# An attention and feed-forward kernel: weight pieces behind the seven-product tiles loaded and converted in halves

## The chip, the cores and the metric

The kernel runs on one core of one Trainium2 chip. The metric is the device time of one execution in microseconds (us), lower is better. The kernel before takes 477.06 us (median of three runs, 477.06 to 477.33). A profiled execution of it, from which all rows below come, took 475.99 us; its span, from the first to the last instruction, is 474.2 us.

## The reference

Three layers follow each other. Inputs of the attention are float32, the weights of the two feed-forward layers are float64.

```python
# attention: 2 x 12 heads, 448 tokens, 64 wide
scores = cap * np.tanh(scale * np.matmul(q, k.transpose(0, 1, 3, 2)) / cap)
attn = exp(scores - max) / (sum + 1e-09);  x = np.matmul(attn, v)   # -> 896 x 768
# first feed-forward layer, w_in 768 x 1024, w_out 1024 x 768
h = x @ w_in;  solu = h * softmax(h);  x = layernorm(solu) * g_ln @ w_out
# second feed-forward layer, w_gate and w_val 768 x 1536, w_out 1536 x 768
g = x @ w_gate
silu = g * (1.0 / (1.0 + np.exp(-g)))
val = x @ w_val
return (silu * val @ w_out).astype(np.float32)
```

The change lies in the second feed-forward layer alone.

## The kernel before

Matrix products work on float32 numbers that are split into a high and a low part: ACT copies the number into the rounded type (`hi_act`), DVE subtracts the copy from the number (`lo_dve`). A product of two such pairs is three matmuls (`mm3`: high by high, high by low, low by high). `split` in the code is the pair hi_act and lo_dve.

A float64 weight comes from memory as 64-bit raw words. `load_shifted` loads them three bytes off, so that the byte with sign and exponent and the word below lie aligned, and `f32_shifted` makes a float32 of them in three steps: a first Prelu on ACT (from the top byte, read as int8), a second Prelu on ACT in place (written as int32), and one SCALAR_TENSOR_TENSOR on DVE, the fill, that brings in the mantissa's bits. An older way, `load64` and `f32`, takes one Abs on ACT and four instructions on DVE, two TENSOR_SCALAR and two SCALAR_TENSOR_TENSOR.

Of the 12 tiles of the second layer's hidden width (fc = 0 to 11, 128 columns of w_gate and w_val each), tiles 1 to 8 are computed with seven products instead of eight on blocks; their order on every engine is written out by hand. Behind them the tiles 9, 10 and 11 are plain: for each of the two token ranges (384 and 512 columns), 18 matmuls for the gate product, 18 for the value product, a Silu on ACT, a product on DVE and a split. There only TensorE's order is fixed by the code; that of ACT and DVE is set by a scheduler when the program is built.

Beside these three tiles the kernel loads what is still missing: the two weights of tile 11 (`load_gv`), and from the second layer's w_out (names `w2_...`) nine pieces (`load_w2`). A piece with a number under 6 is 128 rows of all 768 columns: its left half is split into B11, and right minus left is kept as T1f. Pieces 6, 8 and 10 are the left halves of two chunks each and are split into B21. `early` says which pieces are asked for in which half of which tile. Every piece has 768 words in each of 128 partitions, one raw buffer (tag `raw`, two buffers) and one float32 buffer (tag `f32`, two buffers). All loads are issued in order by SP.

Then `ff2_out` computes the output, again with fewer block products: units named p1, p5, p2 and so on, 18 matmuls of 384 columns each, for token blocks 0, 1, 2 and 6. p1 multiplies A11 by B11, p2 multiplies A12 by B21, p5 works on the sums S1 and T1, p6 on S2 and T2. S2 is written over S1 (tile `so`) by three splits. Beside the first units the right halves of w_out2's lower chunks, three pieces b22, are loaded (`load_b22`, the same two raw buffers), converted the older way (`f32_b22`) and split (`split_b22`); T2, T3, S2 and so on are formed from them and others on DVE, then split.

In the rows, `g` is a weight buffer of gate, value or B parts, `w_raw` a raw w_out2 piece, `b` the float32 b22, `a` the hidden tile and the B22 parts, `p` an accumulator or an output row, `so` the sums S and T. Since a helper records every instruction, all have line L49 in the profile.

Of the kernel before, what the change touches and what calls it, by code (L numbers as in the profile page):

```python
# [5 lines left out]
F32 = mybir.dt.float32  # L6
F32R = mybir.dt.float32r
U32 = mybir.dt.uint32
I64 = mybir.dt.int64
# [47 lines left out]
class Kernel:  # L57
# [566 lines left out]
    def load_gv(self, fc, i):  # L624

        if fc not in self.gvs:
            self.gvs[fc] = [self.g4[m].rearrange("p (u k f) -> p u k f", u=2, f=128)
                            for m in (((0, 1), (2, 3))[fc % 2] if fc else (2, 1))]
        n, w, d = "gv"[i], (self.w_gate, self.w_val)[i], self.gvs[fc][i]
        src = w[:, fc * 128:(fc + 1) * 128].rearrange("(k p) f -> p k f", p=128)  # L630
        raw = self.ee[:, :1536].bitcast(I64) if fc == 0 and i else None
        raw = self.load_shifted(src, f"w{n}_{fc}", raw)
        f = self.f32_shifted(raw, f"w{n}_{fc}").rearrange("p (k f) -> p k f", k=self.KD)
        self.hi_act(d[:, 0], f)
        self.lo_dve(d[:, 1], f, d[:, 0])

# [297 lines left out]
    def split(self, d, src):  # L934

        self.hi_act(d[0], src)
        self.lo_dve(d[1], src, d[0])

    def load_w2(self, fc):

        n = self.HN
        if fc >= self.KD:
            src = self.w_out2[fc * 128:(fc + 2) * 128, :n].rearrange("(f p) d -> p f d", p=128)
        else:
            src = self.w_out2[fc * 128:(fc + 1) * 128, :]
        f = self.f32_shifted(self.load_shifted(src, f"w2_{fc}"), f"w2_{fc}").rearrange("p (f d) -> p f d", f=2)
        if fc >= self.KD:
            for m in range(2):
                self.split(self.B21[fc - self.KD + m], f[:, m])
        else:  # L950
            self.split(self.B11[fc], f[:, 0])
            if fc == len(self.T1f):
                self.T1f.append(f[:, 1])
            self.V.tensor_tensor(self.T1f[fc], f[:, 1], f[:, 0], op=ALU.subtract)

    def load_b22(self, k):

        src = self.w_out2[(self.KD + k) * 128:(self.KD + k + 2) * 128, self.HN:].rearrange("(f p) d -> p f d", p=128)
        self.b22raw[k] = self.load64(src, f"b22_{k}")

    def f32_b22(self, k):

        f = self.B22f[:, k:k + 2].rearrange("p f d -> p (f d)")
        self.f32(self.b22raw.pop(k), f"b22_{k}", f=f)

    def split_b22(self, k):

# [179 lines left out]
    def run(self):  # L1147
# [18 lines left out]
        w = [self.w_in_steps(i) for i in range(KD)]  # L1166
        f, g, hi, lo = zip(*w)
        self.w_steps = [((), f[0][:1], ()), (f[0][1:2], (), f[0][2:] + g[0][:1]), ((), (g[0][1], hi[0]), (lo[0],))]
        for i in range(1, KD):
            a = g[i][:1]  # L1170
# [9 lines left out]
        h = [self.ff1_h(t) for t in range(7)]  # L1180
# [9 lines left out]
        st = self.pool("st", side="right")  # L1190
# [21 lines left out]
        steps = h[1] + h[2][:1] + T[0] + h[2][1:] + h[3][:1] + T[1] + h[3][1:] + wo[0] + h[4][:2] + T[2] + h[4][2:] + wo[1] + h[5][:5] + T3 + h[5][5:] + h[6][:-1] + T4 + h[6][-1:]  # L1212
# [3 lines left out]
        n = self.HN = self.DM // 2  # L1216
        wb, gb = self.wb, _ = self.pool("wb"), self.pool("gb")
# [8 lines left out]
        steps = x2[0][0] + x2[0][1] + wo[2] + x2[1][0][:1] + T5 + x2[1][0][1:] + x2[1][1] + T6  # L1226
        steps += wo[3] + x2[2][0][:1] + x2[0][2] + x2[1][2] + [(0.0, lambda j=j: self.x_sums0(j)) for j in J[:2]]
        for j in range(2, KD):
# [4 lines left out]
            a, b = x2[j]  # L1233
# [27 lines left out]
        self.sg = (self.ee[:, :n], self.ee[:, n:n + 512])  # L1261
        self.T1f = [self.ee[:, n + 512 + n * i:n + 512 + n * (i + 1)] for i in range(3)] + [t1, self.sms]
        self.t1 = t1
        early = {9: ((6, 8), (0,)), 10: ((1,), (2,)), 11: ((3, 4), (5, 10))}
        for fc in range(K2):
            if fc == 0:
                self.ff2_gv_first()
                self.ff2_gv_sevens()
            if fc <= self.KS:
                continue  # L1270
            self.pinned = (nc.tensor,)
            if fc == self.KS + 1:
                d = self.S3f[:, 4:]
                self.V.tensor_tensor(d, d, self.S1f[:, 4:], op=ALU.subtract)
                xR = wb.tile([128, 2688], F32R, name="kR", tag="xR")
                self.B21p[0] = two(xR[:, :1536])
                self.B21[:2] = both(self.B21p[0])
                self.B11[2] = tuple(xR[:, 1536 + n * u:1536 + n * u + n] for u in range(2))
            for i, (N, o) in enumerate(((n, 0), (512, n))):
                if fc == self.KS + 1:  # L1280
                    for m in "hl":
                        self.steps[fc + 1]["GV"[i] + m]()
                elif fc + 1 < K2:
                    self.load_gv(fc + 1, i)
                for c in early[fc][i]:
                    self.load_w2(c)
                self.ff2_gv(fc, N, o)
# [46 lines left out]
```

## Time and profile before

| what | us |
|---|---|
| median of the runs | 477.06 |
| profiled execution | 475.99 |
| its span | 474.2 |
| TensorE (PE) busy | 466.7 (98%) |
| DVE busy | 387.8 (82%) |
| ACT busy | 310.4 (65%) |
| GpSimd (POOL) busy | 38.7 (8%) |

TensorE's granted clock is full in all 40 slices of the span. A busy share is an average over the whole span; in the changed stretch, from about 345 us on, each engine has another share, and the section of rows shows them. A wait in a row stands in brackets: how long the engine was idle just before the instruction, and which engine and tile ended that.

### The profile page before, as it was taken

The numbers are of one execution on the slowest core, as the hardware profiler recorded it, in microseconds if no ns is written. First come the engines' busy times: TensorE is split into PE (matmuls) and PEld (weight loads), VectorE is DVE, ScalarE is ACT, GpSimd is POOL, SyncE is SP. The second block draws the span as 40 slices with busy tenths as digits, with TensorE's granted clock in tenths as the row PEclk, the third lists the DMA queues.
The fourth block names the chain that finished last, engine by engine and source line by source line (L and its number), as shares of the span: only waits on it lengthen the run. The fifth ranks groups of instructions, "written<-read, shape, count | busy, mean of one in ns | idle before, by whom it ended". The sixth has DMA issues, their size and how long they took to land.

```text
span 474.2 us, 7675 instructions
## 1 busy us (share of the span) xinstructions
PE 466.7 (98%) x2970; PEld 384.8 (81%) x2970; DVE 387.8 (82%) x669; ACT 310.4 (65%) x455; POOL 38.7 (8%) x76
## 2 busy tenths in 40 slices
PE   9999999999999999999999999999999999998997
PEld 7444454447888899989989999999999889998996
DVE  3689999987778996866778899989876768999993
ACT  4999999951223799887767766766667778344220
POOL 1011010112000000000012222220000000000000
PEclk9999999999999999999999999999999999999999
DMA  6786575002000225345225444331445757010003
GB/s 181 170 207 153 163 193 153 21 2 88 1 1 0 90 88 165 126 129 180 66 81 185 134 134 132 109 122 37 132 128 155 241 182 221 7 50 18 17 19 132
DMA packets 65060, 52.33 MB, mean 110 GB/s; under 512 B 35584, under 2 KB 61952, under 8 KB 64256
## 3 DMA queue, kind: packets, MB, share of 16 engines
q1 hardware_dynamic: 64992, 51.85, 36.7%
q8 instruction: 23, 0.38, 0.3%
q14 instruction: 13, 0.11, 0.1%
q0 software_dynamic: 32, 0.00, 0.0%
HBM read 49.09 MB, written 2.75 MB: 109 GB/s over the span
## 4 chain that ended last, share of the span: by engine, by line
PE 80%; DVE 10%; DMA 5%; ACT 4%; issue 1%; ACTq 0%; DVEq 0%; SPq 0%
PE x L49 12%; PE h L49 12%; PE p L49 8%; PE g L49 8%; PE pv L49 8%; PE sc L49 7%; PE b L49 6%; PE c L49 6%; PE S L49 4%; DMA w_raw<-in_moe_w_out_dram 3%; PE e L49 3%; DVE b L49 2%; ACT w L49 2%; PE v L49 2%; DVE so L49 1%; PE lt L49 1%
## 5 line engine op out<-in xcount | busy, mean ns | idle before, releaser
L49 PE MATMUL g<-x,g 128*128 128x448 f32 (+2 forms) x288 | 62.2, 365 | 0.0
L49 PE MATMUL h<-wi,x 128*128 128x512 f32 x252 | 59.2, 393 | 0.0
L49 PEld LDWEIGHTS g<-x,g 128*128 128x128 f32 x288 | 53.1, 188 | 5.4 <-ACT ee L49 0.3
L49 PEld LDWEIGHTS h<-wi,x 128*128 128x128 f32 x252 | 46.8, 188 | 11.3 <-issue 1.5
L49 ACT ACTIVATE P<-sc,consts 112x896 f32<-112x896 f32 x48 | 45.4, 1010 | 3.8 <-PE sc L49 2.2
L49 ACT ACTIVATE P<-P,consts 112x3584 f32<-112x3584 f32 (+1 forms) x13 | 39.7, 3060 | 0.1
L49 PE MATMUL pv<-P,v 112*32 112x448 f32 x384 | 38.5, 540 | 0.0
L49 PEld LDWEIGHTS sc<-ks 64*112 64x112 f32 x288 | 23.3, 171 | 18.3 <-issue 8.4
L49 PE MATMUL sc<-ks 64*112 64x448 f32 x288 | 35.8, 379 | 0.3
L49 PE MATMUL x<-lB,wo 128*128 128x256 f32 (+1 forms) x192 | 35.2, 337 | 0.0
L49 PEld LDWEIGHTS x<-lB,wo 128*128 128x128 f32 x192 | 29.6, 189 | 3.4
L49 PE MATMUL b<-a,g 128*128 128x448 f32 x144 | 31.9, 366 | 0.0
L49 ACT ACTIVATE ee<-h,sms 128x512 f32<-128x512 f32 x14 | 9.5, 685 | 33.2 <-DVE sms L49 33.2
L49 PEld LDWEIGHTS pv<-P,v 112*32 112x32 f32 x384 | 12.2, 110 | 23.0 <-issue 20.9
L49 PE MATMUL v<-x,g 128*128 128x384 f32 (+1 forms) x144 | 30.4, 362 | 0.3 <-DVE g L49 0.3
L49 PEld LDWEIGHTS b<-a,g 128*128 128x128 f32 x144 | 27.0, 188 | 2.3 <-DVE ee L49 0.2
L49 PEld LDWEIGHTS v<-x,g 128*128 128x128 f32 x144 | 26.0, 188 | 3.5 <-DVE g L49 0.7
L49 PE MATMUL x<-lA,wo 128*128 128x384 f32 x144 | 27.2, 338 | 0.0
L49 PEld LDWEIGHTS x<-lA,wo 128*128 128x128 f32 x144 | 25.2, 188 | 0.5
L49 POOL COPY sm<-tr 32x14 f32<-32x14 f32 x48 | 15.0, 312 | 93.1 <-DVE tr L49 91.6
L49 PE MATMUL S<-P,ones 112*32 112x448 f32 x192 | 22.4, 549 | 0.0
L49 DVE TENSOR_TENSOR x<-x,x 128x448 fp32r<-128x448 f32 (+3 forms) x26 | 15.3, 588 | 8.3 <-ACT x L49 7.6
(273 smaller groups left out, 967.6 us busy)
## 6 DMA issues: line engine op xcount, KB each, us to landing
wg_raw<-in_moe_w_gate_dram SPq DMA_DIRECT2D x12, 765.8 KB, 4.3
wv_raw<-in_moe_w_val_dram SPq DMA_DIRECT2D x11, 765.8 KB, 4.7
wi_raw<-in_moe_w_in_dram SPq DMA_DIRECT2D x6, 1024.0 KB, 7.7
w_raw<-in_moe_w_out_dram SPq DMA_DIRECT2D x6, 767.6 KB, 4.2
wo_raw<-in_moe_w_out_dram SPq DMA_DIRECT2D x6, 512.0 KB, 3.5
wo_raw<-in_moe_w_out_dram SPq DMA_DIRECT2D x6, 510.5 KB, 3.6
v<-in_v_dram SPq DMA_DIRECT2D x24, 112.0 KB, 4.0
kq<-in_k_dram SPq DMA_DIRECT2D x22, 112.0 KB, 3.0
```

Of the source, the lines that this page charges most:

```text
L49: i = f(*a, **k)
```

## The change

Behind the seven-product tiles the two raw tiles are taken once, as four halves of 384 words. `load_halves` loads a piece in two loads, each into the next of the four halves, and converts each half by itself: two Prelus and a fill over 384 columns each. The float32 buffer is still one of 768 columns, and the splits that follow are as before. Both `load_w2` and `load_gv` for tile 11 use it. `early` asks for the pieces in another order. The three b22 pieces are loaded shifted and converted by two Prelus and one fill of 768 columns, no longer by Abs and four DVE instructions.

```diff
@@ load_gv
-        raw = self.ee[:, :1536].bitcast(I64) if fc == 0 and i else None
-        raw = self.load_shifted(src, f"w{n}_{fc}", raw)
-        f = self.f32_shifted(raw, f"w{n}_{fc}").rearrange("p (k f) -> p k f", k=self.KD)
+        if fc:
+            f = self.load_halves([src[:, 3 * h:3 * h + 3] for h in range(2)], f"w{n}_{fc}")
+        else:
+            raw = self.ee[:, :1536].bitcast(I64) if i else None
+            f = self.f32_shifted(self.load_shifted(src, f"w{n}_0", raw), f"w{n}_0")
+        f = f.rearrange("p (k f) -> p k f", k=self.KD)
@@ new
+    def load_halves(self, src, name):
+
+        f = self.st[0].tile([128, 768], F32, name=name, tag="f32", bufs=2)
+        steps = [{}, {}]
+        for h in range(2):
+            raw = self.halves.pop(0)
+            self.halves.append(raw)
+            self.load_shifted(src[h], f"{name}_{h}", raw)
+            self.shifted_steps(steps[h], "", lambda raw=raw: raw, lambda h=h: f[:, 384 * h:384 * h + 384])
+        for o in steps:
+            for w in "12f":
+                o["w" + w]()
+        return f
@@ load_w2
-        n = self.HN
+        n, w = self.HN, self.w_out2
         if fc >= self.KD:
-            src = self.w_out2[fc * 128:(fc + 2) * 128, :n].rearrange("(f p) d -> p f d", p=128)
+            src = [w[(fc + h) * 128:(fc + h + 1) * 128, :n] for h in range(2)]
         else:
-            src = self.w_out2[fc * 128:(fc + 1) * 128, :]
-        f = self.f32_shifted(self.load_shifted(src, f"w2_{fc}"), f"w2_{fc}").rearrange("p (f d) -> p f d", f=2)
+            src = [w[fc * 128:(fc + 1) * 128, h * n:(h + 1) * n] for h in range(2)]
+        f = self.load_halves(src, f"w2_{fc}").rearrange("p (f d) -> p f d", f=2)
@@ load_b22, f32_b22
-        self.b22raw[k] = self.load64(src, f"b22_{k}")
+        self.b22raw[k] = self.load_shifted(src, f"b22_{k}")
-        self.f32(self.b22raw.pop(k), f"b22_{k}", f=f)
+        raw, o = self.b22raw.pop(k), {}
+        self.shifted_steps(o, "b", lambda: raw, lambda: f)
+        for w in "12f":
+            o["wb" + w]()
@@ run
-        early = {9: ((6, 8), (0,)), 10: ((1,), (2,)), 11: ((3, 4), (5, 10))}
+        early = {9: ((0, 1), (2,)), 10: ((3,), (6,)), 11: ((4, 8), (5, 10))}
...
+                self.halves = [t[:, a:a + 384] for t in (st.tile([128, 768], I64, name=f"h{m}", tag="raw", bufs=2)
+                                                         for m in range(2)) for a in (0, 384)]
```

The load queue, SP, from behind the last load of the seven-product tiles to the last w_out2 piece, before (`w_6_raw` is the raw buffer of piece 6, `wg_raw` and `wv_raw` those of tile 11's gate and value weights):

```order
L177 DMA w_6_raw<-in_moe_w_out_dram 128x2x3069
L177 DMA w_8_raw<-in_moe_w_out_dram 128x2x3069
L173 DMA w_0_raw<-in_moe_w_out_dram 128x6141
L177 DMA wg_raw<-in_moe_w_gate_dram 128x6x1021
L173 DMA w_1_raw<-in_moe_w_out_dram 128x6141
L177 DMA wv_raw<-in_moe_w_val_dram 128x6x1021
L173 DMA w_2_raw<-in_moe_w_out_dram 128x6141
L173 DMA w_3_raw<-in_moe_w_out_dram 128x6141
L173 DMA w_4_raw<-in_moe_w_out_dram 128x6141
L173 DMA w_5_raw<-in_moe_w_out_dram 128x6141
L177 DMA w_10_raw<-in_moe_w_out_dram 128x2x3069
```

The same place now; `h_3484` and `h_3485` are the two raw tiles, each of two halves, and the pieces are 0, 1, 2, gate, 3, value, 6, 4, 8, 5 and 10:

```order
L173 DMA h_3484<-in_moe_w_out_dram 128x3069 x2
L173 DMA h_3485<-in_moe_w_out_dram 128x3069 x2
L173 DMA h_3484<-in_moe_w_out_dram 128x3069 x2
L177 DMA h_3485<-in_moe_w_gate_dram 128x3x1021 x2
L173 DMA h_3484<-in_moe_w_out_dram 128x3069 x2
L177 DMA h_3485<-in_moe_w_val_dram 128x3x1021 x2
L173 DMA h_3484<-in_moe_w_out_dram 128x3069 x2
L173 DMA h_3485<-in_moe_w_out_dram 128x3069 x2
L173 DMA h_3484<-in_moe_w_out_dram 128x3069 x2
L173 DMA h_3485<-in_moe_w_out_dram 128x3069 x2
L173 DMA h_3484<-in_moe_w_out_dram 128x3069 x2
```

Eleven loads have become 22; the value weights of tile 11 are sixth and piece 5 is tenth in both.

DVE at piece 5, beside the last value product (`v_384`), before (`w_5` is the float32 piece, `g_0_1928` the buffer of B11's chunks 4 and 5):

```order
L49 SCALAR_TENSOR_TENSOR w_5_3784<-w_5_raw,w_5_3784 128x768
L49 TENSOR_TENSOR w_5_3784<-w_5_3784 128x384
L49 TENSOR_TENSOR ee<-v_384_3820,ee 128x512
L49 TENSOR_TENSOR g_0_1928<-w_5_3784,g_0_1928 128x384
L49 TENSOR_TENSOR s_2487<-s_2487,ee 128x384
```

And now:

```order
L49 SCALAR_TENSOR_TENSOR w_5_3811<-h_3485,w_5_3811 128x384
L49 TENSOR_TENSOR g_0_1928<-w_5_3811,g_0_1928 128x384
L49 TENSOR_TENSOR w_5_3811<-w_5_3811 128x384
L49 SCALAR_TENSOR_TENSOR w_10_3823<-h_3484,w_10_3823 128x384 x2
L49 TENSOR_TENSOR g_1_1929<-w_10_3823,g_1_1929 128x384 x2
L49 TENSOR_TENSOR ee<-v_384_3855,ee 128x512
```

The low part of piece 5 comes right behind its second fill, and piece 10 is done ahead of the eviction of the last value product.

DVE at the second and third b22 piece, before (`b_3850` is the float32 b22, `a_2485` its split parts):

```order
L49 TENSOR_TENSOR so<-sms,so 128x384
L49 TENSOR_TENSOR g_1_1929<-w_10_3793,g_1_1929 128x384 x2
L49 TENSOR_TENSOR so<-w_5_3784,so 128x384
L49 TENSOR_SCALAR b_3850<-b_3850 128x768 x2
L49 SCALAR_TENSOR_TENSOR b_3850<-b_2_raw,b_3850 128x768 x2
L49 TENSOR_SCALAR b_3850<-b_3850 128x768 x2
L49 SCALAR_TENSOR_TENSOR b_3850<-b_4_raw,b_3850 128x768 x2
L49 TENSOR_TENSOR a_2485<-b_3850,a_2485 128x2x384 x3
```

And now:

```order
L49 TENSOR_TENSOR so<-sms,so 128x384
L49 TENSOR_TENSOR so<-w_5_3811,so 128x384
L49 SCALAR_TENSOR_TENSOR b_3885<-b_2_raw,b_3885 128x768
L49 SCALAR_TENSOR_TENSOR b_3885<-b_4_raw,b_3885 128x768
L49 TENSOR_TENSOR a_2485<-b_3885,a_2485 128x2x384 x3
```

Each piece has one DVE instruction in place of four; behind the three splits the order of DVE is the same as before.

## Rows read from the trace of the kernel before

**Rows 1.** TensorE in order of time: start, us, instruction [idle before, released by].
```profile
377.05 0.52 PE L49 MATMUL v<-x,g 128*128 128x384 f32 x2
377.91 3.05 PE L49 MATMUL v<-x,g 128*128 128x384 f32 x16 [0.34 <-DVE g L49]
380.79 4.28 PE L49 MATMUL g<-x,g 128*128 128x512 f32 x18
...
388.99 1.23 PE L49 MATMUL p<-a,a 128*128 128x384 f32 x6
...
392.68 0.62 PE L49 MATMUL p<-g,a 128*128 128x384 f32 x2 [0.66 <-DVE g L49]
393.14 1.20 PE L49 MATMUL p<-a,a 128*128 128x384 f32 x6
...
396.26 1.20 PE L49 MATMUL p<-a,a 128*128 128x384 f32 x6
...
404.58 1.42 PE L49 MATMUL p<-g,a 128*128 128x384 f32 x6
405.84 1.20 PE L49 MATMUL p<-kR,kK 128*128 128x384 f32 x6
...
430.80 0.51 PE L49 MATMUL p<-t,so 128*128 128x384 f32 x2
433.35 0.98 PE L49 MATMUL p<-t,so 128*128 128x384 f32 x4 [2.04 <-DVE so L49]
434.17 1.21 PE L49 MATMUL p<-so 128*128 128x384 f32 x6
```

**Rows 2.** Chain that ended last: start, us, what (the second load).
```profile
350.56 6.12 DMA w_raw<-in_moe_w_out_dram
```

**Rows 3.** Load queue SP in order of time, merged: first issues; b22's three.
```profile
349.16 1.77 SPq L177 DMA_DIRECT2D w_raw<-in_moe_w_out_dram  x2
...
391.00 8.91 SPq L111 DMA_DIRECT2D b_raw<-in_moe_w_out_dram  x3
```

**Rows 4.** ACT in order of time: first Prelu of the first piece.
```profile
353.75 0.98 ACT L49 ACTIVATE w<-w_raw,consts 128x768 f32<-128x768 int8 x1 [1.21 <-DMA w_raw<-in_moe_w_out_dram]
```

**Rows 5.** DVE in order of time, merged.
```profile
392.08 0.55 DVE L49 TENSOR_TENSOR g<-w,g 128x384 fp32r<-128x384 f32 x1
...
396.32 1.15 DVE L49 TENSOR_SCALAR b<-b 128x768 f32<-128x768 f32 x2 [0.42 <-ACT b L49]
397.51 1.95 DVE L49 SCALAR_TENSOR_TENSOR b<-b_raw,b 128x768 uint32<-128x768 uint32 x2
...
411.77 2.69 DVE L49 TENSOR_TENSOR a<-b,a 128x768 fp32r<-128x768 f32 x3
...
432.35 3.56 DVE L49 TENSOR_TENSOR so<-s,so 128x768 fp32r<-128x768 f32 x4
```

**Rows 6.** ACT by shape, whole span: count | busy us, mean ns | idle before.
```profile
L49 ACT ACTIVATE w<-w_raw,consts 128x768 f32<-128x768 int8 x9 | 9.0, 995 | 6.2 <-DMA w_raw<-in_moe_w_out_dram 4.9 <-DVE w L49 1.1 <-ACT a L49 0.2
L49 ACT ACTIVATE w<-w,consts 128x768 int32<-128x768 f32 x9 | 8.4, 931 | 0.1
...
L49 ACT ACTIVATE wo<-wo_raw,consts 128x512 f32<-128x512 int8 x6 | 4.4, 758 | 0.0
...
L49 ACT ACTIVATE wo<-wo,consts 128x512 int32<-128x512 f32 x6 | 4.2, 718 | 0.1
...
L49 ACT ACTIVATE g<-wv 128x768 fp32r<-128x768 f32 x3 | 2.5, 846 | 1.3 <-DVE wv L49 1.3
```

**Rows 7.** Busy us of two stretches: PE, PEld, DVE, ACT, POOL, clock, DMA share, GB/s.
```profile
349.00:391.00 42.00, 41.66 (x206) 36.98 (x205) 28.66 (x44) 30.46 (x43) 0.00 (x0) 1.00 0.61 197
391.00:433.00 42.00, 39.65 (x226) 38.70 (x224) 40.11 (x61) 24.60 (x40) 0.00 (x0) 1.00 0.27 86
```

**Rows 8.** The page's DMA issues: count, KB each, median us from issue to landing.
```profile
w_raw<-in_moe_w_out_dram SPq DMA_DIRECT2D x6, 767.6 KB, 4.2
...
wo_raw<-in_moe_w_out_dram SPq DMA_DIRECT2D x6, 510.5 KB, 3.6
```

## The prediction

> **What bounds the kernel now.** I read the views in this order: the page's busy shares, TensorE's instructions in order of time behind the seven-product tiles, the chain that ended last over the same stretch, then the load queue, ACT and DVE there. Only the stretch from about 345 us on is changed; in front of it the order of every engine is the same.
>
> TensorE is busy 98% of the span, so a gain can only come out of its pauses. Ends of matmuls are modelled, so I compare starts [rows 1]. Undisturbed, a unit of 18 matmuls of 384 columns takes 396.26 - 393.14 = 3.12, that is 0.173 for one matmul and 1.04 for six. Four places take longer. The value product of the last tile, v_11: 380.79 - 377.05 = 3.74, lost 0.62 (waits for the low part of its weights, "DVE g"). The first unit of the output product, p1_0: 393.14 - 388.99 = 4.15, lost 1.03 (low part of w_out2's chunk 5, again "DVE g"). The last six of p2_0: 405.84 - 404.58 = 1.26, lost 0.22. The first six of p6_0: 434.17 - 430.80 = 3.37, lost 2.33 (waits for "DVE so", the low part of S2). Together 4.20 us; elsewhere in the stretch the starts follow each other at these distances. So the change can give back at most 4.2 us here, 0.9% of the span, unless it slows something.
>
> Behind the first three pauses stand the loads. The chain of waits shows one load after another: a piece queued behind another needs 6.12 us from its issue at 350.56, so it lands at 356.68 [rows 2]; the first piece, issued at 349.16, is converted from 353.75 on [rows 3, 4]. The twelfth load (b22's first) is issued at 391.00: 41.8 us for eleven pieces, 3.8 for one, because a raw buffer is free again only after its piece has landed, been through two ACT passes and been filled on DVE. Behind the fourth pause stands DVE: it converts the three b22 pieces with two TENSOR_SCALARs (1.15) and two SCALAR_TENSOR_TENSORs (1.95) each from 396.32 on, has filled the last at 411.77 and then runs through without a rest to the four "so" splits at 432.35, the first of which p6_0 waits for [rows 5].
>
> **The change part by part.** *Durations.* ACT's first Prelu takes 0.995 at 768 columns and 0.758 at 512, the second 0.931 and 0.718 [rows 6]. Going on by the same slope, 384 columns take 0.64 and 0.61. The 512-column values are the upper bound, half of the 768-column ones (0.50, 0.47) the lower; I take the slope, since two rows carry it. A fill of 768 columns is 0.97 (1.95 for two), and a DVE pass over 384 columns 0.55 (the split at 392.08) [rows 5], which I take for the half fill.
>
> *Cost of halving.* Eleven pieces: ACT gets 2 x (0.64 + 0.61) - 1.93 = 0.57 more for each, 6.3 in all, on top of 30.46 busy of the 42 us between 349 and 391 [rows 7]: 36.8, still below 42. DVE gets 2 x 0.55 - 0.97 = 0.13 each, 1.4 on 28.66. SP issues eleven loads more; two took 1.77 with the wait between them [rows 3], so one takes under 0.9, less than the distance at which halves can land. None of it is on TensorE's path as long as both stay below 42. On ACT, what now stands behind a Prelu that waits for its half is the Silu of a gate product; TensorE needs that PSUM bank only eight accumulators later, so the wait is covered.
>
> *The loads.* A half alone: 510 KB land in 3.6 and 768 KB in 4.2 [rows 8], so 383 KB in about 3.3. Behind each other, whole pieces land 356.68 - 353.7 = 3.0 apart. For halves I bound the distance: by bytes alone 1.5; with everything kept that doesn't shrink between 768 and 510 KB, 3.0 - 0.6 x 385 / 258 = 2.1. No row shows two loads of this size behind each other; I take 1.75, near the middle, for both rows count alike. A slot's own round (3.3 landing, 0.64 + 0.61 + 0.55 converting) is 5.1, over four slots 1.3, so the stream of bytes sets the pace, with 0.45 x 4 us to spare for waiting in ACT's and DVE's queues. The k-th half then lands at 349.16 + 3.3 + 1.75 (k - 1).
>
> The Trainium skill speaks against this part: "DMA: Bandwidth & Descriptors", section "Measured (HBM→SBUF, 128 partitions, SWDGE, issued from GpSimd)", asks for transfers of at least 1 MiB, to reach three quarters of the peak rate; its fit in "Anatomy of one DMA — SWDGE (gpsimd) path" has 2.0 us fixed plus the bytes at 436 GB/s, by which halves that hid nothing would come 2.9 apart (an estimate). The queued piece that lands 3.0 behind the other speaks against paying all of that in a stream.
>
> *v_11.* Its second half is the 12th: 371.7, then 0.64 + 0.61 + 0.55 and the split, 0.85 on ACT [rows 6] and about 0.97 on DVE: 375.3. TensorE asks for it with the third matmul, 377.05 + 0.35 = 377.4. Margin 2.1, the 0.62 goes.
>
> *p1_0.* Chunk 5 is the tenth piece before and now, the new order of the others leaves it there; its second half is the 20th: 385.7. Now its split stands right behind the fill on DVE, no longer behind the eviction of v_11: 0.64 + 0.61 + 0.55 + 0.5 + 0.55 gives 388.6. TensorE asked for it with the 17th matmul, 388.99 + 16 x 0.173 = 391.8, and asks 0.62 earlier now, at 391.1. Margin 2.5, the 1.03 goes. Chunk 10 is done by about 392.5, p2_0's last six start behind 402: the 0.22 goes.
>
> *p6_0.* The raw tiles become free with chunk 5 (387.5) and chunk 10 (391). The first b22 piece follows the 22nd half (389.2) by 3.0 and lands at 392.2, the second is issued at 391 and lands at 395.3, the third waits for the first's conversion (two Prelus and a fill, 2.9): issued 395.1, landed 399.3, filled 402.2 instead of 411.77. On DVE each piece keeps one fill of four instructions: 1.15 + 0.97 = 2.1 less, 6.4 for three; on ACT each gets about 1.0 more (one Abs becomes two Prelus), in a stretch where ACT has 24.60 us of work in 42 [rows 7], so it is hidden. DVE's block from 411.77 to the first "so" split's end (432.35 + 0.95 = 433.3) is 21.5 long. Started at about 403.4, behind the first split on ACT, it ends at 424.9. TensorE, 1.87 earlier, asks at 430.80 - 1.87 + 0.35 = 429.3. Margin 4.4, the 2.33 goes.
>
> *What is late next.* Every margin is over 2 us, but with halves 1.9 apart v_11's falls to 0.4, p1_0's to zero and p6_0's to about 1. Small new waits of 0.3 to 0.4 in all are what I leave in. Sum: 4.20 - 0.35 = 3.85. The profiled execution took 475.99 with a span of 474.2; its time would be 472.1. The median of the runs shown is 477.06, 1.07 above it; the same difference gives 473.2.
>
> **The rivals.**
> *The fourth wait stays.* DVE works in order, and if b22's last piece is late (its load hangs on chunk 10, the fill and the second Prelu), or the block is held up by evictions, p6_0 pauses nearly as before, while the first three waits go. For it: DVE was the only gapless engine there. Against: 8 us earlier start. The gain is 1.87, the time 475.2.
>
> *ACT becomes the bound.* At the upper bound for half Prelus, ACT gets 11 x (2 x 1.48 - 1.93) = 11.3 more, 41.8 of 42: every wait then goes through to the chunks, and by the margins some 1.5 us of the pauses return: 474.6. With more still, what is gained is lost: 476.7, no change. Against it: the slope of the two sizes.
>
> *Halves cost nearly what pieces cost (slower).* Place: the load queue from 349 on. At a distance of 2.2 the 12th half lands at 376.7, its split is done at 380.3: 2.9 lost at v_11; the 20th lands at 394.3, done at 397.1 against 391.1 + 2.9: 3.1 lost at p1_0; p6_0, later by as much, has no wait. 6.0 against 4.2: slower by 1.8, 478.9. It decides from about 2.1 on. Against it: 3.0 for a whole piece, and my own bound ends at 2.1. By the Trainium skill's fit (same page, "Anatomy of one DMA"), with 2.9 between halves, this rival would hold, and by more; the queued piece speaks against that, as said.
>
> **How the numbers follow.** Forecast (3 to 4.2 us gained): 0.62. The fourth wait or ACT keep part of it (1 to 3 gained): 0.22. No change, below 0.2% or 0.95 us, about what a measurement of this kernel can tell: 0.08. Slower: 0.08, of which the load queue has most. The faster side is 0.62 + 0.22 = 0.84. The range begins at 472.4, 4.2 gained and 0.45 for scatter (the three runs differ by 0.27), and ends at 476.0, behind the rival with the fourth wait and short of no change.
>
> **What would show it.** Right: v_11, p1_0 and p2_0 without pause, units of 3.12 throughout; halves landing 1.5 to 1.9 apart; the first half Prelu at 0.64; b22 filled for the last time near 402; p6_0 without pause. Wrong: pauses on "DMA h" in ACT's queue with halves 2.1 or more apart; ACT full between 349 and 391; TensorE waiting for "DVE so" near 429; a pause in a place that had none.

## The result and the profile after

The changed kernel takes 471.27 us (four runs, 470.45 to 472.02) against 477.06 (476.92 to 477.33) for the kernel before: a ratio of 0.9878, interval 0.986 to 0.9895. That is 5.8 us faster. The forecast was 3.85 faster, 473.2, with a range from 472.4; the sign was right, the size too small, and the time lies below the range.

The profiled execution, though, took 472.02 us against the forecast's 472.1 for it, with a span of 470.3. The engines' shares of the chain that ended last, before:

```profile
PE 80%; DVE 10%; DMA 5%; ACT 4%; issue 1%; ACTq 0%; DVEq 0%; SPq 0%
```

After, with the page's busy shares above it:

```profile
PE 465.7 (99%) x2970; PEld 383.8 (82%) x2970; DVE 381.4 (81%) x671; ACT 316.2 (67%) x480; POOL 38.7 (8%) x76
...
PE 99%; DVE 1%; issue 0%
```

No load is left in the chain. TensorE in order of time (start, us, instruction), at the four places of [rows 1]:

```profile
377.24 3.28 PE L49 MATMUL v<-x,g 128*128 128x384 f32 x18
380.36 4.28 PE L49 MATMUL g<-x,g 128*128 128x512 f32 x18
...
388.56 1.23 PE L49 MATMUL p<-a,a 128*128 128x384 f32 x6
...
391.71 1.20 PE L49 MATMUL p<-a,a 128*128 128x384 f32 x6
...
403.15 1.20 PE L49 MATMUL p<-g,a 128*128 128x384 f32 x6
404.19 1.20 PE L49 MATMUL p<-kR,kK 128*128 128x384 f32 x6
...
429.15 1.20 PE L49 MATMUL p<-t,so 128*128 128x384 f32 x6
430.19 1.20 PE L49 MATMUL p<-so 128*128 128x384 f32 x6
```

v_11 takes 380.36 - 377.24 = 3.12 (3.74 before), p1_0 391.71 - 388.56 = 3.15 (4.15), the last six of p2_0 and the first six of p6_0 1.04 each (1.26 and 3.37). No row of the stretch carries a wait. From tile 9's first matmul to the end of the span before took 474.2 - 344.97 = 129.2 us and after takes 470.3 - 345.18 = 125.1: the 4.2 of the four pauses, to a tenth.

The two windows of [rows 7], the half Prelus and those of b22 (as in [rows 6]), and the page's line of the halves' loads (as in [rows 8]):

```profile
349.00:391.00 42.00, 42.00 (x209) 37.67 (x209) 30.24 (x58) 35.68 (x70) 0.00 (x0) 1.00 0.71 213
391.00:433.00 42.00, 42.00 (x245) 42.00 (x244) 38.60 (x58) 26.77 (x42) 0.00 (x0) 1.00 0.21 69
```

```profile
L49 ACT ACTIVATE w<-h,consts 128x384 f32<-128x384 int8 x18 | 11.3, 636 | 4.8 <-DMA h<-in_moe_w_out_dram 4.8
L49 ACT ACTIVATE w<-w,consts 128x384 int32<-128x384 f32 x18 | 10.5, 606 | 0.0
...
L49 ACT ACTIVATE b<-b_raw,consts 128x768 f32<-128x768 int8 x3 | 3.0, 997 | 0.0
```

```profile
h<-in_moe_w_out_dram SPq DMA_DIRECT2D x18, 383.6 KB, 3.6
```

TensorE fills both windows. ACT has 35.68 of 42, DVE 30.24 in the first: neither is the bound. DVE at b22 and at the `so` splits (as in [rows 5]), then ACT at the second and third b22 piece:

```profile
395.76 0.96 DVE L49 SCALAR_TENSOR_TENSOR b<-b_raw,b 128x768 uint32<-128x768 uint32 x1 [1.17 <-ACT b L49]
...
402.98 0.96 DVE L49 SCALAR_TENSOR_TENSOR b<-b_raw,b 128x768 uint32<-128x768 uint32 x1 [0.91 <-ACT b L49]
404.86 0.96 DVE L49 SCALAR_TENSOR_TENSOR b<-b_raw,b 128x768 uint32<-128x768 uint32 x1 [0.92 <-ACT b L49]
405.97 2.81 DVE L49 TENSOR_TENSOR a<-b,a 128x768 fp32r<-128x768 f32 x3 [0.15 <-ACT a L49]
...
426.67 3.55 DVE L49 TENSOR_TENSOR so<-s,so 128x768 fp32r<-128x768 f32 x4
```

```profile
395.64 0.83 ACT L49 ACTIVATE so<-s 128x768 fp32r<-128x768 f32 x1
...
399.04 0.84 ACT L49 ACTIVATE so<-s 128x768 fp32r<-128x768 f32 x1
...
400.60 0.48 ACT L49 ACTIVATE p<-p 128x384 f32<-128x384 f32 x1
400.97 1.00 ACT L49 ACTIVATE b<-b_raw,consts 128x768 f32<-128x768 int8 x1
402.01 0.94 ACT L49 ACTIVATE b<-b,consts 128x768 int32<-128x768 f32 x1
402.85 1.00 ACT L49 ACTIVATE b<-b_raw,consts 128x768 f32<-128x768 int8 x1
```

The last b22 fill ends at 405.8 (411.8 before, 402.2 forecast): the second piece has landed at 395.79, but its Prelu starts at 400.97. In ACT's order eight copies for the `so` splits (`so<-s` and others, the first at 395.64) and two evictions (`p<-p`) stand ahead of it. The first `so` split ends at 426.67 + 0.95 = 427.6, and TensorE asks at 429.15 + 0.35 = 429.5.

### The profile page after: what moved, and what is told of

It reads as the page before. It is cut to its first block, busy times and chain, and to the rows that moved or that the text cites. A ratio compares the mean times of both kernels' runs of the same rounds, so it can differ in the third digit from the quotient of the medians.

```text
span 470.3 us, 7732 instructions
## 1 busy us (share of the span) xinstructions
PE 465.7 (99%) x2970; PEld 383.8 (82%) x2970; DVE 381.4 (81%) x671; ACT 316.2 (67%) x480; POOL 38.7 (8%) x76
## 4 chain that ended last, share of the span: by engine, by line
PE 99%; DVE 1%; issue 0%
PE p L49 17%; PE g L49 13%; PE x L49 12%; PE h L49 12%; PE pv L49 8%; PE sc L49 7%; PE b L49 6%; PE v L49 6%; PE c L49 6%; PE S L49 4%; PE e L49 3%; PE lt L49 1%; PE T L49 1%; PE warm L49 1%; DVE ks L49 0%; PE d L49 0%
## 5 line engine op out<-in xcount | busy, mean ns | idle before, releaser
L49 PE MATMUL v<-x,g 128*128 128x384 f32 (+1 forms) x144 | 30.1, 362 | 0.0
```

Of the source, the lines that this page charges most:

```text
L49: i = f(*a, **k)
```

## The experiments

The forecast for the profiled execution holds, so the question is why the median gained 1.9 more than was forecast. The first four runs weigh two theories: that the changed part gives what its pauses showed and the rest is chance between executions (A), or that the pauses of before are usually longer than in the execution that was profiled (B). Each ratio is to runs of the kernel before on the same chip; runs taken together share these.

**Before, again** (no edit).

> The kernel before, unchanged, for more executions and a second profile. Theory A (the change takes away the four pauses of 4.2 us and nothing else; the rest of the 5.8 lies in parts that it doesn't touch): the pauses are again 4.0 to 4.5 in sum, while the start (full clock from 6.4 us in the first profile) and the distance of the 448-column matmuls between 264 and 343 us (0.2027 in the first profile of before, 0.2067 in that of after) come out differently from the first profile, and the times of single runs spread by 1 us or more. Theory B (typical executions of before have longer pauses than the profiled one): the four pauses sum to 5.0 us or more, with start and distance as in the first profile.

Measured: 476.48 us (12 runs), ratio 0.9988 (0.9969 to 1.0006). This profiled execution took 477.17, with a span of 475.4. TensorE at p6_0, and the window behind it (busy PE, PEld, DVE, ACT, POOL, granted clock):

```profile
430.43 0.51 PE L49 MATMUL p<-t,so 128*128 128x384 f32 x2
432.95 0.98 PE L49 MATMUL p<-t,so 128*128 128x384 f32 x4 [2.01 <-DVE so L49]
433.77 1.64 PE L49 MATMUL p<-so 128*128 128x384 f32 x6
435.21 3.44 PE L49 MATMUL p<-t,so 128*128 128x384 f32 x12
438.48 1.21 PE L49 MATMUL p<-so 128*128 128x384 f32 x6
```

```profile
433.00:438.00 5.00, 5.00 (x20) 5.00 (x21) 5.00 (x7) 1.16 (x3) 0.00 (x0) 0.66 0.00 0
```

The pause is the one of [rows 1], 2.01 against 2.04 idle. What is new stands behind it: the granted clock goes from its full level, 2.4 GHz, to the half one, 1.2 GHz, from 434.34 to 437.76 by the clock's records, and matmuls that take 0.173 elsewhere come 0.32 apart. p6_0 and p6_1 lose 3.57 + 0.32 = 3.89 here against 2.33 in the execution of the forecast, 1.56 more. Neither theory holds as it stands. All losses behind 345 us sum to 6.5 here against 4.2, as B had it, but only 0.69 of the 2.25 more are longer waits, all of them ahead of p6_0; the 1.56 are the half clock. And the start differs, as A had it: the clock is full from 4.26 us instead of 6.38.

The fall can be counted without a profile. At half the clock for 3.42 of 475.4 us the mean granted clock of a run is 0.996. Of 75 runs of the kernel before on three chips, 39 have 0.996 or less, with a median of 477.23 us; 36 have 0.998 or more, with 475.66. The difference is 1.57 (interval 1.15 to 2.03), the same as in the trace; chip by chip it is 1.3, 1.7 and 1.8.

**After, again** (no edit).

> The changed kernel again. Both theories: no pause behind 345 us. Theory A: spans of single runs between 468.7 and 471.5 in steps that go with the start and the 448-column distance, and the second profile has one of the two otherwise than the first. Theory B: start and distance as in the first profile, span within 0.3 of 470.3.

Measured: 471.45 us (6 runs), ratio 0.9884 (0.9862 to 0.9906). No pause, and a mean clock of 1.0 in all six runs. Against the runs of before without the fall, on the three chips, that is 475.66 - 471.45 = 4.2 faster, against those with it 5.8. On this chip alone it is 4.5 and 5.8.

**The halves alone.**

```diff
@@ load_b22, f32_b22 (after)
-        self.b22raw[k] = self.load_shifted(src, f"b22_{k}")
+        self.b22raw[k] = self.load64(src, f"b22_{k}")
-        raw, o = self.b22raw.pop(k), {}
...
+        self.f32(self.b22raw.pop(k), f"b22_{k}", f=f)
```

> Halves and new order as in the change, but the b22 pieces by Abs and four DVE instructions as before. Theory A: v_11, p1_0 and p2_0 without pause (1.87 gained); p6_0's pause remains in part, since the b22 pieces start only 2 to 3 us earlier and DVE still does 6.4 us more: 0 to 2.5 of the 2.33 lost, in all 1.9 to 4.2 gained on the kernel before in the pauses. Rival (the halves are the whole gain): no pause at all.

Measured: 472.37 us, ratio 0.9903 (0.9881 to 0.9925). One pause is left, at p6_0, 0.47 lost (the median is 0.9 above that of the change; the profile shows only these 0.47):

```profile
428.85 0.51 PE L49 MATMUL p<-t,so 128*128 128x384 f32 x2
429.54 0.97 PE L49 MATMUL p<-t,so 128*128 128x384 f32 x4 [0.18 <-DVE so L49]
```

So the halves alone take away most of p6_0's pause as well, since b22's loads start earlier (the first at 387.30, not 391.00); the mean clock is 0.999 or 1.0 in all runs.

**b22's Prelus alone** (the same lines, the other way round, in the kernel before).

> Whole pieces in the old order, b22 by two Prelus and a fill. Theory A: v_11, p1_0 and p2_0 pause as before (1.87), p6_0 has none: 2.3 gained in the pauses. Rival (p6_0's pause goes with the loads, not with DVE's work): p6_0 still pauses 1 us or more.

Measured: 473.71 us, ratio 0.9934 (0.9911 to 0.9957). p6_0 has no pause; p1_0 loses 0.97 and v_11 0.78, and 0.55 goes at the gate product ahead of v_11, 2.3 in all. The mean clock is 0.999 or 1.0: behind pauses of these lengths (0.66 us idle at most) none of these six runs has a fall. The kernel before without its fall, 475.66, less the 4.2 - 2.3 = 1.9 that went, is 473.8.

The next runs weigh two theories of the fall: its cause is the long pause (C), or it has nothing to do with it (D).

**Before, with p6_0's pause filled** by 18 small products of ones into the accumulator that p6_0 then starts anew.

```diff
+            if nm == "p6_0":
+                self.keep_warm(18, acc)
             self.products(acc, A, B() if callable(B) else B, t, start, evict is not None)
```

> The kernel before with 18 small matmuls of ones (64 columns, into the accumulator that p6_0 clears afterwards) just ahead of p6_0, so that TensorE works through most of the pause there; DVE's chain is untouched. Theory C (behind the long pause at p6_0 TensorE's granted clock falls to half in most executions of before, and that price of about 1.5 us goes with the pause): p6_0 starts its real work at the same time as before, but the clock is full behind it, the runs' mean clock is 0.999 to 1.000 and the median is 475.0 to 475.9. Rival D (the fall has nothing to do with the pause): mean clocks of 0.995 to 0.996 stay in half of the runs, median 476.5 to 477.5.

Measured: 475.83 us (12 runs), ratio 0.9987 (0.9963 to 1.0012): the median lies where C put it, but the interval holds no change too, so the time decides nothing. The mean clock is 0.996 in 3 of 12 runs, where C wanted none and D half; of before beside them it is 0.996 or less in 13 of 23. That leans to C and could still be chance. What the three have is open; this kernel keeps the pauses at p1_0, and in its profile TensorE was idle there twice within six matmuls, 0.94 and 0.66.

**After, with a pause put back:** nine DVE maxima that change no number, ahead of the S2 splits.

```diff
         def s2(k):
+            for i in range(9 if k == 0 else 0):
+                V.tensor_tensor(S3f[:, i % KD], S3f[:, i % KD], S3f[:, i % KD], op=ALU.max)
             self.split(
```

> The changed kernel with nine idle passes on DVE (384 columns, the maximum of S3 with itself, 4.2 us in all) ahead of S2's splits, so that p6_0 pauses again for about 2.3 us; the loads and conversions are as in the change. Theory C: half or more of the runs have a mean clock of 0.995 to 0.997, the profile may show half clock for some 3.4 us behind p6_0, median 474.0 to 475.5 (471.4 + 2.3 + about 1.5 where it falls). Rival D: mean clocks stay at 0.999 to 1.000 and the median is 473.5 to 473.9.

Measured: 473.61 us, ratio 0.9924 (0.9902 to 0.9945). The pause came out shorter than planned, 1.41 idle and 1.71 lost, and no run shows a fall; the time lies in D's range:

```profile
432.36 0.98 PE L49 MATMUL p<-t,so 128*128 128x384 f32 x4 [1.41 <-DVE so L49]
```

C spoke of a pause of 2.3, so this leaves C and D undecided; a longer pause follows below.

**After, with the pieces in the old order** (`early` of before), and **before, with the new order** (`early` of after).

> The change with the pieces asked for in the order of before (6, 8, 0, 1, 2, 3, 4, 5, 10). If the order doesn't matter, as the prediction has it: no pause, 471.0 to 471.9. Rival (the new order carries part): v_11 pauses by 0.5 or more, 472 or more.

Measured: 471.36 us, ratio 0.9884 (0.9862 to 0.9907), no pause. With halves the order makes no difference.

> The kernel before with only the new order of the pieces, whole loads, b22 the older way. As the prediction has it the order alone gains nothing: v_11 and p1_0 pause by 1.5 us or more in sum, p6_0 by 1 to 2.4, median 475.5 to 477.5. Rival (the order carries the gain): 474 or less.

Measured: 475.86 us (12 runs), ratio 0.9987 (0.997 to 1.0005). Against the expectation v_11 and p6_0 have no pause; p1_0 has a long one, and the window of 4 us from 393 on has this clock:

```profile
389.47 0.69 PE L49 MATMUL p<-g,a 128*128 128x384 f32 x3
392.38 1.47 PE L49 MATMUL p<-g,a 128*128 128x384 f32 x3 [2.22 <-ACT g L49]
393.65 2.12 PE L49 MATMUL p<-a,a 128*128 128x384 f32 x6
395.57 1.14 PE L49 MATMUL p<-kR,a 128*128 128x384 f32 x3
```

```profile
393.00:397.00 4.00, 4.00 (x14) 4.00 (x15) 3.58 (x6) 3.50 (x7) 0.00 (x0) 0.57 0.77 226
```

The fall has moved with the pause: half clock from 393.15 to 396.56, 41 us earlier than in the kernel before, and full clock at p6_0. p1_0 loses 3.16, and p1_1, which has no wait, 1.38. Of 12 runs 11 have a mean clock of 0.996 or less. This speaks for C.

**After, with a longer pause, idle and filled:** the same edit with twelve maxima, and beside it the same with `keep_warm(24, acc)` ahead of p6_0. DVE works alike in both.

> The changed kernel with twelve idle-making DVE passes (maxima of S3 with itself, 0.47 us apart, which change no number) ahead of the four S2 splits, three more than in the run before that left TensorE idle for 1.41 us. Each adds 0.47 us, so TensorE is idle about 2.8 us at p6_0, longer than the kernel before there. Theory C (TensorE's clock falls to half behind an idle time of about 2 us and more, and costs about 1.5 us beyond it): profile with half clock behind p6_0's pause, mean clock 0.997 or below in most runs, time 471.3 + 3.1 + 1.5 = 475.9 us. Theory D (the fall has nothing to do with the pause's length): mean clock 0.998 or above in nearly all runs, 474.4 us.

Measured: 475.78 us (12 runs), ratio 1.0001 (0.9982 to 1.0021). TensorE, and the window behind:

```profile
428.87 0.51 PE L49 MATMUL p<-t,so 128*128 128x384 f32 x2
432.59 1.25 PE L49 MATMUL p<-t,so 128*128 128x384 f32 x4 [3.21 <-DVE so L49]
433.63 2.12 PE L49 MATMUL p<-so 128*128 128x384 f32 x6
435.55 2.69 PE L49 MATMUL p<-t,so 128*128 128x384 f32 x12
```

```profile
433.00:438.00 5.00, 5.00 (x22) 5.00 (x21) 5.00 (x8) 1.58 (x4) 0.00 (x0) 0.66 0.00 0
```

> The same twelve DVE passes, and ahead of p6_0's products TensorE gets 24 small products of zeros into the accumulator that p6_0 then starts anew (48 matmuls of 64 columns, 3.1 us by the run in which 18 of them took 2.31). DVE is late by as much as in the run beside it, but TensorE isn't idle. Theory C: no fall of the clock, about 474.4 us, 1.5 us less than the run beside it although TensorE's useful work waits as long. Theory D: both runs take the same time, with the same clocks.

Measured: 474.46 us (12 runs), ratio 0.9971 (0.9956 to 0.9987).

```profile
427.91 3.01 PE L49 MATMUL p<-const-float32-1.0 128*64 128x64 f32 x48
430.85 1.32 PE L49 MATMUL p<-t,so 128*128 128x384 f32 x6
432.01 1.21 PE L49 MATMUL p<-so 128*128 128x384 f32 x6
```

Idle, the mean clock is 0.996 or less in 11 of 12 runs (0.993, about two falls, in two of them); filled, it is 0.999 or 1.0 in all 12, and the time is 1.32 less (interval 0.5 to 2.5), though the S2 splits come as late, 26.3 us behind the first b22 split in both. Both times are within 0.15 of what C gave (with luck: its sum had 2.8 idle, not 3.21), and D, which wanted the same clocks and times of both, falls. The products that wait are the same; what TensorE does meanwhile differs, small products of ones (the expectation says zeros) or nothing. Counted by its matmuls the fall costs 1.56 in the idle profile, as in that of before. The wait itself was 0.4 longer in the idle profile than in the filled one, so the 1.32 between the medians need not be the fall alone.

## Why the prediction was right in sign and short in size

**The four pauses: right.** All four went, 4.2 us, by the steps given: halves instead of pieces for v_11, p1_0 and p2_0, the earlier end of DVE's block for p6_0. The 0.35 left in for small new waits was not needed.

**The prices of the halves: right; their pace: right by luck.** Half Prelus measured 0.636 and 0.606 (forecast 0.64 and 0.61), a half fill 0.55, ACT 35.7 (36.8), DVE 30.2 (30.1). The 22 halves landed between 352.51 and 387.39, on average 1.66 apart (1.75 forecast, 2.1 the point from which the slower rival decides). But "the stream of bytes sets the pace" does not hold. In ten of the eleven pieces the second half landed 0.9 to 1.4 us behind the first, under the 1.5 that the prediction had for the bytes alone. And every load from the fifth on was issued 0.03 us after the fill of the half four places ahead of it, whose raw buffer it takes over. The first two fills on DVE, then the fifth and the sixth issue on SP:

```profile
354.20 0.56 DVE L49 SCALAR_TENSOR_TENSOR w<-h,w 128x384 uint32<-128x384 uint32 x1
356.79 0.56 DVE L49 SCALAR_TENSOR_TENSOR w<-h,w 128x384 uint32<-128x384 uint32 x1 [2.03 <-ACT w L49]
```

```profile
354.79 0.33 SPq L173 DMA_DIRECT2D h<-in_moe_w_out_dram  x1
```

```profile
357.38 0.33 SPq L173 DMA_DIRECT2D h<-in_moe_w_out_dram  x1
```

So the round of a raw buffer sets the pace. It took 6.7 us on average (the first buffer's five rounds, 349.38 to 382.83), since a half was filled 2.3 to 4.6 us after it had landed, not 1.8; the prediction had 5.1. Over four buffers that is 1.67. The Trainium skill's fit for loads that GpSimd issues ("DMA: Bandwidth & Descriptors", "Anatomy of one DMA — SWDGE (gpsimd) path") has 2.0 us fixed plus the bytes; as an estimate from it, halves that hid nothing would have come 2.9 apart. For halves queued on SP the 0.9 to 1.4 decide against that.

**The margins: right but for one.** v_11's low part is done at 375.7 and asked for at 377.6, 1.9 (2.1 forecast); p1_0's at 389.0 against 391.3, 2.3 (2.5). p6_0 has 1.9 instead of 4.4: ACT's order, with the `so` copies and two evictions ahead of the second b22 Prelu, was not in the working. It cost nothing here, but without the shortened conversion the same chain is late by 0.47 (the run with the halves alone).

**The step that failed** is the last of the sum: the median is "1.07 above it; the same difference gives 473.2". The difference between the profiled execution and the median was carried over as a constant, as if it came from outside the change. It was the fall of the clock behind p6_0's pause, which the profiled execution didn't have and 39 of the 75 runs do. It belongs to the pause and goes with it. The sum should have had a fifth term: 1.57 in the runs that have the fall. Then 477.06 - 4.2 - 1.57 = 471.3, against 471.27 measured, closer than the scatter of the runs warrants. That the runs behind the 477.06 had the fall is likely but not shown, for their clocks are not on record: they took 476.92 to 477.33, the runs known to have it have a median of 477.23, and of the 36 known to be without it four took 476.92 or more. The page showed a full clock in all 40 slices, and the prediction has no term for the clock; it was one execution out of two kinds.

**The rivals** each fell by a row: no "DVE so" wait is left at p6_0; ACT isn't full; the halves came 1.66 apart.

## What to carry to other kernels

When the profiled execution is faster or slower than the median by more than the runs scatter, find out what differs before adding the difference as a constant: it can hang on the very wait that a change removes. Behind the pauses of TensorE of 2.0 to 3.2 us here stood, in half to nearly all of the executions, another 1.6 us at the half clock, so such a pause can be worth more than its idle time. Where the wait itself can't be removed, products that nobody needs can keep the clock: they did in all 12 runs at the pause of 3.2, and in 9 of 12 at the pause of 2.0. A half that stood queued landed 0.9 to 1.4 us behind the half before it, against 3.1 and more from its issue when it came alone; so halving a piece whose consumer waits for the whole of it was nearly free here, where ACT and DVE had room for the longer conversion.

## What the runs showed of the hardware

*The clock behind a pause.* Of the kernel whose longest pause was 1.41 us idle in its profile, none of 6 runs had a fall; with 2.01 to 2.04, 39 of 75; with 2.22, 11 of 12; with 3.21, 11 of 12. In three of the last 24 runs the mean clock, 0.992 or 0.993, is that of two falls. Each of the three falls in a profile lasted 3.4 us (434.34 to 437.76, 393.15 to 396.56, 433.10 to 436.51), though TensorE had work without a gap in it. The Trainium skill ("TensorE: Matmul & The Clock Gate", "HAM oscillation — how this bites in real kernels") tells of work that starts at the half clock behind a wait for loads. The traces here agree in that the half clock stands behind a wait (0.57 to 0.66 granted over 4 to 5 us), but the waits were for DVE and ACT, and the work began at the full clock and fell 0.5 to 1.4 us later. Why a pause of 2.0 brings the fall in one execution and not in the next was not settled.

*Two differences that cancelled.* Parts that the change doesn't touch differed between the two profiled executions. TensorE at the start and at the end of the seven-product tiles, before:

```profile
264.71 1.58 PE L49 MATMUL e<-a,w 128*128 128x448 f32 x7
...
344.97 1.23 PE L49 MATMUL g<-x,g 128*128 128x384 f32 x6
```

And after:

```profile
263.34 2.02 PE L49 MATMUL e<-a,w 128*128 128x448 f32 x9
...
345.18 1.03 PE L49 MATMUL g<-x,g 128*128 128x384 f32 x5
```

The execution of after was 1.37 us ahead at the first of these and 0.21 behind at the second. Its clock rose to full at 3.56 us instead of 6.38, which would give half of 2.82, 1.4 us, at the start (an estimate); and between the two rows its matmuls of 448 columns came 206.7 ns apart instead of 202.7, both at a full granted clock. The same changed kernel showed the other pace in its second profile (202.7, full clock at 6.69), so neither belongs to the change. They cancelled to 0.2 us, so it is partly luck that the two spans gave the right 4 us all the same. What sets the pace was not tried.
